# The second channel product of two token tiles by Strassen's algorithm, in a fused attention and mixer kernel in fp32

## The chip, the cores and the metric

The kernel is one program on 1 core of a Trainium2 chip. Its time is the device time of one execution in microseconds (us), the median of three runs. The engines are PE (TensorE, with PEld for its weight loads), DVE (VectorE), ACT (ScalarE), POOL (GpSimd, which here issues DMAs) and SP (SyncE, which issues most DMAs).

## The reference, cut to what matters

```python
# x: 4 batches x 448 tokens x 768, the result of sigmoid attention and a gated convolution
h  = np.maximum(xt @ w_tok1, 0.0) @ w_tok2          # mixes tokens, xt = x transposed
u  = x + h.transpose(0, 2, 1)
h2 = np.maximum(u @ w_ch1, 0.0) @ w_ch2             # w_ch1 768 x 1536, w_ch2 1536 x 768
out = (u + h2).astype(np.float32)
```

The change lies in the last two lines: `u @ w_ch1` is the first channel product, the product with `w_ch2` the second. There are 1792 tokens.

## The kernel before

The program runs through attention, the gated projections, the token mix and at last the channel products. It computes everything transposed: channels lie on the 128 partitions, tokens in the columns. An fp32 product is made of three matmuls on fp32r operands: every operand is split into a high part (ACT copies it to fp32r) and a low part (DVE subtracts the high part), and high x high, low x high and high x low are added in PSUM. An array of 768 channels has KD = 6 blocks of 128, the 1536 hidden channels have KF = 12 blocks, called `fc`.

The 1792 tokens go in four tiles of 512, 512, 384 and 384 (`TILES`), called 0 to 3. For tiles 0 and 1, `ch1(t, fc)` makes one block of hidden channels (18 matmuls, L745), splits its ReLU (`split`, L92 and L94), and `ch2(t, fc)` adds that block's share of all six output blocks in six PSUM banks (`pso`, tags `o0` to `o5`, 18 matmuls, L772). Their calls alternate, `ch2` one block behind `ch1`. After `fc` = 11 DVE adds `u` to each bank (L778, tile `ur`) and SP stores the sum.

For tiles 2 and 3 together the first channel product is made by Strassen's algorithm (in Winograd's form, seven block products instead of eight): the two tiles are the two columns of a block matrix, the two halves of the 768 input channels its rows, and the hidden blocks 2i and 2i+1 the two rows of the weights. What it needs is made beside tile 1, at places that `beside` lists by the block `fc` of `ch1(1, fc)`: `sums(i)` forms the four sums of weights for pair i on DVE and ACT and stores all seven operands in the HBM scratch `fscr` (L892, L912); `turned_load(k)` and `turned(k)` load u and form the seven operands of the tokens for block k of 3 (L932, L936, L940). Then `seven(i)` makes the seven products of pair i, 9 matmuls each (`product`, L976), in two PSUM banks (`h`), with weights that POOL loads from `fscr` six products ahead (`form_load`, L968, tiles `wf` in the six `xs` buffers), and DVE adds them up (L993).

The second channel product of tiles 2 and 3 is not by Strassen before: `ch2(2, fc)` follows each `seven`, two blocks behind, and `ch2(3, fc)` comes last, with hidden blocks that went to the scratch `rscr` and come back (`r_load`, `r_split`). Tiles 2 and 3 take 12 x 18 matmuls each there, on 384 columns.

From `with tc.manual_schedule()` on, each engine's order is the order of the code; ahead of it a scheduler sets it.

Of the kernel before, what the change touches and what calls it, by code (L numbers as in the profile page):

```python
# [34 lines left out]
def tile_kernel(ctx, tc, qT, kT, v, w_val, conv_w, w_out, w_tok1, w_tok2, w_ch1, w_ch2, out):  # L35
# [39 lines left out]
    rscr = dram.tile([KF, P, NJ], F32, name="rscr")  # L75

    def f(ap):
        return ap.bitcast(F32)
# [786 lines left out]
    with tc.high_priority(-CHAN_LOW):  # L865
        for fc in range(CHAN_HELD + 1, KF):
            dec_ch(fc)
    forms = ("a11", "s2", "s1", "s4", "s3", "a12", "a22")
    spot = {name: n for n, name in enumerate(("a11", "a12", "a22", "s1", "s2", "s3", "s4"))}
    room = []  # L870
    bform = {}

    def form_room():
        if not room:
            fc = form_room.at
            form_room.at += 1
            if 0 < fc < CHAN_LATE:
                get = w_tile if fc < CHAN_HELD else wo_tile
                room.extend(get().rearrange("p (c m) -> p c m", c=2) for _ in range(2))
            else:  # L880
                t = rp["p" if fc else "a"].tile([P, 2, 2, HALF], F32R, tag=f"wch{fc}_0", bufs=1, name="bf")
                room.extend(t[:, n] for n in range(2))
        return room.pop(0)

    form_room.at = 0

    def keep_weights(fc):
        for a in range(2):
            w = f(wch[fc][0][a])
            for n, h in enumerate((0, 1) if fc % 2 == 0 else (1,)):  # L890
                at = spot[("a11", "a12")[h] if fc % 2 == 0 else "a22"]
                nc.sync.dma_start(fscr[fc // 2, at, :, a], w[:, h * HALF : (h + 1) * HALF])  # L892

    def sums(i):
        keep_weights(2 * i)
        keep_weights(2 * i + 1)
# [4 lines left out]
        add = lambda o, x, y, op=ALU.add: nc.vector.tensor_tensor(out=o, in0=x, in1=y, op=op)  # L901
        for w, fc in ((wa, 2 * i), (wb, 2 * i + 1)):
            add(w, f(wch[fc][0][0]), f(wch[fc][0][1]))
        s = [f(su[:, n]) for n in range(4)]
        add(s[0], wb[:, :HALF], wb[:, HALF:])
        add(s[1], s[0], wa[:, :HALF], ALU.subtract)
        add(s[2], wa[:, :HALF], wb[:, :HALF], ALU.subtract)
        add(s[3], wa[:, HALF:], s[1], ALU.subtract)
# [4 lines left out]

    ub = {}

    def turned_load(k):
        at = [None] * 6
        if k == KH - 1:
            spare = [rp["a"].tile([P, 4, NJ], F32, tag="raw", bufs=2, name="ub") for _ in range(2)]
            at = [spare[n // 4][:, n % 4] for n in range(6)]  # L920
        ub[k] = [u_load(t, k + h, "ub", at[2 * n + t - 2]) for n, h in enumerate((0, KH)) for t in (2, 3)], at[4:]

    def turned(k):
        (b11, b12, b21, b22), t = ub.pop(k)
        if t[0] is None:
            t = [both.tile([P, W], F32, tag="gate", bufs=6, name="ut")[:, :NJ] for _ in range(2)]
        t1, t2 = t
        to = {}

        def high(name, src):  # L930
            to[name] = src, form_room()
            nc.scalar.activation(out=to[name][1][:, 0], in_=src, func=AF.Copy)  # L932

        def low(name):
            src, x = to.pop(name)
            nc.vector.tensor_tensor(out=x[:, 1], in0=src, in1=f(x[:, 0]), op=ALU.subtract)  # L936
            bform[name, k] = x

        def sub(o, x, y):
            nc.vector.tensor_tensor(out=o, in0=x, in1=y, op=ALU.subtract)  # L940

        high("b11", b11)
        sub(t1, b12, b11)
        high("t1", t1)
        low("b11")
        sub(t2, b22, t1)
# [4 lines left out]
        sub(b12, b22, b12)  # L951
# [4 lines left out]
        sub(t1, b21, t2)  # L956
# [4 lines left out]
    queue = [(i, name) for i in range(KF // 2) for name in forms]  # L961
    held_f = {}

    def form_load():
        if queue:
            i, name = queue.pop(0)
            t = both.tile([P, 2, HALF], F32R, tag="xs", bufs=KD, name="wf")
            nc.gpsimd.dma_start(t, fscr[i, spot[name]])  # L968
            held_f[i, name] = t

    def product(i, name, x):
        ps = psc.tile([P, 512], F32, tag="h", bufs=2, name="psm")[:, :NJ]
        w = held_f.pop((i, name))
        for k in range(KH):
            for n, (a, c) in enumerate(((0, 0), (1, 0), (0, 1))):
                nc.tensor.matmul(  # L976
                    ps, w[:, a, k * P : (k + 1) * P], bform[x, k][:, c],
                    start=k == 0 and n == 0, stop=k == KH - 1 and n == 2,
                )
        form_load()  # L980
        return ps

    def seven(i):
        def spare():
            return both.tile([P, W], F32, tag="gate", bufs=6, name="um")[:, :NJ]

        def out(ps):
            t = spare()
            nc.scalar.activation(out=t, in_=ps, func=AF.Copy)  # L989
            return t  # L990

        def add(o, x, y):
            nc.vector.tensor_tensor(out=o, in0=x, in1=y, op=ALU.add)  # L993

        m1 = out(product(i, "a11", "b11"))
        u = spare()
        add(u, product(i, "s2", "t2"), m1)
        m5 = out(product(i, "s1", "t1"))
        v = spare()
        add(v, u, m5)  # L1000
        add(v, product(i, "s4", "b22"), v)
        nc.sync.dma_start(rscr[2 * i], v)
        add(u, product(i, "s3", "t3"), u)
        add(m5, u, m5)
        nc.sync.dma_start(rscr[2 * i + 1], m5)
        r = rp["a"].tile([P, 2, 2, NJ], F32R, tag="raw", bufs=2, name="rr")
        add(m1, product(i, "a12", "b21"), m1)
        split(r[:, 0, 0], r[:, 0, 1], m1, relu=True)
        add(u, product(i, "a22", "t4"), u)
        split(r[:, 1, 0], r[:, 1, 1], u, relu=True)  # L1010
        for n in range(2):
            r_t[2, 2 * i + n] = [r[:, n, c] for c in range(2)]

    back = {}

    def r_load(fc):
        if fc < KF:
            back[fc] = both.tile([P, W], F32, tag="gate", bufs=6, name="rl")[:, :NJ]
            nc.sync.dma_start(back[fc], rscr[fc])

    def r_split(fc):
        if fc < KF:
            r = rp["p"].tile([P, 2, W], F32R, tag="r", bufs=2, name="r")
            r = [r[:, c, :NJ] for c in range(2)]
            split(*r, back.pop(fc), relu=True)
            r_t[3, fc] = r
# [10 lines left out]
    cut = order.index((ch2, 0, KF - 1)) + 1  # L1037
    for fn, t, fc in order[:cut]:
# [7 lines left out]
    with tc.manual_schedule():  # L1046
        beside = {1: (sums, 0), 2: (sums, 1), 3: (sums, 2), 4: (turned_load, 0, sums, 3), 5: (turned, 0)}
        beside |= {6: (sums, 4), 7: (turned_load, 1, sums, 5), 8: (turned, 1), 9: (turned_load, 2), 11: (turned, 2)}
        for fn, t, fc in order[cut:]:
            fn(t, fc)  # L1050
            if fn is ch1:
                todo = beside.get(fc, ())
                for n in range(0, len(todo), 2):
                    todo[n](todo[n + 1])
            if fn is ch1 and fc == KF - 1:
# [64 lines left out]
```

## Time and profile before

| | |
|---|---|
| median of three runs | 709.95 us (709.52 to 710.09) |
| the profiled execution, its own time | 710.43 us |
| span of its profile, first to last instruction | 708.7 us |
| instructions | 11027 |
| busy: PE, PEld | 701.8 us (99%), 574.3 us (81%) |
| busy: DVE, ACT, POOL | 481.0 us (68%), 305.4 us (43%), 88.9 us (13%) |
| DMA | 128.16 MB, mean 181 GB/s |

Times in the profile count from the start of the span. Shares of busy time are means over stages with different limits, so the stages are read one by one; the last 170 us, from the second half of tile 1 on, are those the change rewrites.

### The profile page before, as it was taken

The page shows a single profiled execution, that of the slowest core. Times are in us where ns is not written, and L with a number is a line of the kernel's source. Part 1 is how long each engine was busy: PE and PEld are TensorE (multiplying, and loading weights), DVE is VectorE, ACT ScalarE, POOL GpSimd, SP SyncE. Part 2 cuts the span into 40 slices and gives each one's busy share as a digit, 9 for nine tenths or more (in the row PEclk, how much of TensorE's full clock was granted, in tenths as well). Part 3 has the DMA queues.
Part 4 walks back from the last instruction along what each step waited for, and adds up shares of the span by engine and source line. Part 5 has one row for each costly group of instructions (what it writes and reads, how often), then busy time and mean ns, then how long its engine had stood idle before and what let it go on. Part 6 is the DMA issues. An engine that isn't in the chain of part 4 may idle for free.

```text
span 708.7 us, 11027 instructions
## 1 busy us (share of the span) xinstructions
PE 701.8 (99%) x4210; PEld 574.3 (81%) x4210; DVE 481.0 (68%) x789; ACT 305.4 (43%) x454; POOL 88.9 (13%) x128
## 2 busy tenths in 40 slices
PE   8999999999999999999999999999999999999997
PEld 3344444699999999999988888888888899999997
DVE  1799776479899988976878999747774543233222
ACT  5899888337426435524733344402322211111110
POOL 0000110003214212400350000000000232220000
PEclk9999999999999999999999999999999999999999
DMA  9847999413346333335895444337967696663533
GB/s 290 261 132 234 278 288 282 145 54 85 53 158 198 72 110 114 86 118 160 240 305 202 158 159 174 98 126 297 331 218 244 190 296 185 189 192 122 176 100 111
DMA packets 102212, 128.16 MB, mean 181 GB/s; under 512 B 35072, under 2 KB 89104, under 8 KB 102160
## 3 DMA queue, kind: packets, MB, share of 16 engines
q1 hardware_dynamic: 90672, 90.40, 42.3%
q0 software_dynamic: 11056, 36.61, 16.2%
q8 instruction: 33, 0.54, 0.3%
q10 hardware_dynamic: 432, 0.46, 0.2%
q14 instruction: 19, 0.16, 0.1%
HBM read 83.98 MB, written 37.16 MB: 171 GB/s over the span
## 4 chain that ended last, share of the span: by engine, by line
PE 93%; DVE 3%; DMA 2%; ACT 1%; issue 1%; SPq 0%; DVEq 0%; ACTq 0%
PE psd L359 24%; PE pso L772 23%; PE psh L745 12%; PE psm L976 9%; PE pss L281 9%; PE psy L296 8%; PE pst L423 4%; PE pst L436 4%; DMA raw<-w_ch 1%; ACT ga L283 1%; DMA k<-kT 0%; DMA out<-ur 0%; DVE dec_a L135 0%; DVE x2T L440 0%; DVE ub L940 0%
## 5 line engine op out<-in xcount | busy, mean ns | idle before, releaser
L283 ACT ACTIVATE ga<-pss,bias_s 128x896 f32<-128x896 f32 x84 | 83.4, 1003 | 19.9 <-PE pss L281 19.3
L359 PE MATMUL psd<-gv,wo 128*128 128x448 f32 x432 | 88.0, 362 | 0.0
L359 PE MATMUL psd<-xs,w 128*128 128x448 f32 x432 | 87.7, 362 | 0.0
L359 PEld LDWEIGHTS psd<-xs,w 128*128 128x128 f32 x432 | 80.8, 187 | 6.0 <-issue 0.7
L359 PEld LDWEIGHTS psd<-gv,wo 128*128 128x128 f32 x432 | 81.0, 187 | 5.4
L281 PE MATMUL pss<-q,k 64*64 64x448 f32 x672 | 79.1, 542 | 1.1 <-ACT ga L283 0.7
L296 PE MATMUL psy<-ga,v 64*64 64x448 f32 x672 | 77.6, 536 | 0.0
L329 DVE SCALAR_TENSOR_TENSOR gate<-xb,cw,gate 128x448 f32<-128x448 f32 x96 | 75.0, 781 | 2.6
L281 PEld LDWEIGHTS pss<-q,k 64*64 64x64 f32 x672 | 26.0, 134 | 40.2 <-issue 29.6
L296 PEld LDWEIGHTS psy<-ga,v 64*64 64x64 f32 x672 | 25.7, 133 | 37.4 <-issue 35.9
L968 POOL DMA_DIRECT2D wf<-fscr x42 | 22.2, 528 | 238.8 <-PE psh L745 167.1
L135 DVE SCALAR_TENSOR_TENSOR dec_a<-raw,dec_a 128x768 int32<-128x768 int32 (+2 forms) x38 | 33.5, 881 | 20.8 <-ACT dec_a L123 20.8
L123 ACT ACTIVATE dec_a<-dec_a,exp_b 128x768 int32<-128x768 int32 (+3 forms) x39 | 33.0, 858 | 33.0 <-DVE dec_a L120 33.0
L993 DVE TENSOR_TENSOR um<-psm,um 128x384 f32<-128x384 f32 x30 | 16.7, 556 | 43.9 <-PE psm L976 42.9
L394 POOL COPY pl<-st 128x1024 uint16<-128x1024 uint16 x21 | 30.7, 1460 | 103.9 <-ACT gate L340 50.8
L370 ACT ACTIVATE gv<-gate 128x448 fp32r<-128x448 f32 x24 | 13.9, 578 | 56.8 <-DVE gate L368 56.7
L976 PE MATMUL psm<-bf,wf 128*128 128x384 f32 x162 | 35.9, 335 | 0.3 <-ACT um L989 0.3
L94 DVE SCALAR_TENSOR_TENSOR r<-psh,r 128x512 fp32r<-128x512 f32 x22 | 15.0, 688 | 30.3 <-ACT r L92 30.3
L772 PE MATMUL pso<-r,wo 128*128 128x512 f32 (+1 forms) x162 | 35.0, 371 | 0.0
L772 PEld LDWEIGHTS pso<-r,wo 128*128 128x128 f32 x162 | 29.6, 188 | 4.2
L772 PE MATMUL pso<-r,w 128*128 128x512 f32 (+1 forms) x144 | 30.9, 369 | 0.0
L92 ACT ACTIVATE r<-psh 128x512 fp32r<-128x512 f32 x22 | 12.9, 591 | 40.9 <-PE psh L745 40.9
(200 smaller groups left out, 1282.7 us busy)
## 6 DMA issues: line engine op xcount, KB each, us to landing
raw<-w_ch SPq DMA_DIRECT2D x24, 768.0 KB, 4.4
wf<-fscr POOLq DMA_DIRECT2D x42, 384.0 KB, 4.7
v<-v SPq DMA_DIRECT2D x24, 224.0 KB, 6.4
uscr<-x2T POOLq DMA_DIRECT2D x24, 224.0 KB, 2.4
q<-qT SPq DMA_DIRECT2D x23, 224.0 KB, 4.5
k<-kT SPq DMA_DIRECT2D x22, 224.0 KB, 4.6
raw<-w_out POOLq DMA_DIRECT2D x6, 768.0 KB, 8.1
fscr<-sum_h SPq DMA_DIRECT2D x6, 768.0 KB, 3.4
```

The lines of the kernel that those rows point to most:

```text
L123: nc.scalar.activation(out=t["a"], in_=t["a"], func=AF.Relu, scale=8.0, bias=exp_b)
L135: nc.vector.scalar_tensor_tensor(out=t["a"], in0=hi, scalar=-0x80000000, in1=t["a"], op0=ALU.bitwise_and, op1=ALU.bitwise_or)
L281: nc.tensor.matmul(ps[cols, j, :S], k[rows, keys], q[rows], start=True, stop=True)
L283: nc.scalar.activation(out=a, in_=ps[:, :, :S], func=AF.Sigmoid, bias=bias_s, scale=QK_SCALE)
L296: nc.tensor.matmul(y_t[i + h][cols, :S], v_t[i][rows, c, cols], a[rows, j], start=c == 0, stop=c == NB - 1)
L329: nc.vector.scalar_tensor_tensor(out=acc, in0=x[:, t : t + S], scalar=w, in1=acc, op0=ALU.mult, op1=ALU.add)
L359: nc.tensor.matmul(ps[:, :S], w(a, kk), s[:, c, :], start=kk == 0 and n == 0, stop=kk == KD - 1 and n == 2,)
L394: nc.gpsimd.tensor_copy(back.rearrange("p (n h) -> p h n", h=2), st.rearrange("p h c d -> p h (c d)"))
L423: nc.tensor.matmul(ps[:, :HALF], a, x[:, m], start=n == 0, stop=n == len(mm) - 1)
L745: nc.tensor.matmul(ps[:, :n_t], wch[fc][0][a][:, kk * P : (kk + 1) * P], us_t[t, kk][:, c, :], start=kk == 0 and n == 0, stop=kk == KD - 1 ...
L772: nc.tensor.matmul(acc[j][:, :n_t], wch[fc][1][a][:, j * P : (j + 1) * P], r[c], start=fc == 0 and n == 0, stop=fc == KF - 1 and n == 2,)
L976: nc.tensor.matmul(ps, w[:, a, k * P : (k + 1) * P], bform[x, k][:, c], start=k == 0 and n == 0, stop=k == KH - 1 and n == 2,)
```

## The change

The second channel product of tiles 2 and 3 is also made by Strassen's algorithm: `second(j)` makes output blocks j and j + 3 of both tiles by seven products of 18 matmuls (six pairs of hidden blocks, three matmuls each), for j = 0, 1, 2. That is 3 x 7 x 18 = 378 matmuls on 384 columns in place of 432; `ch2(2, ...)`, `ch2(3, ...)`, `rscr`, `r_load` and `r_split` are gone. The pairs of hidden blocks are now f and f + 6.

- `sums_second(i)`, new: DVE forms the operands of the second weights for pair i (two sums of 128x768, four of 128x384) and SP stores seven operands in the new scratch `gscr`, laid out so that a product can load one block. Each store moves 128 x 3 runs of 128 floats (512 bytes).
- `first_pairs(i)` replaces `seven(i)`: all six pairs come one after the other, with no `ch2` between them. It adds up the products, takes the ReLU, and forms the seven operands of the hidden blocks (`rform`), each split in a high and a low part; the last of these steps run beside the next pair (`tail`).
- `second(j)` loads its weights unsplit (`load_2`), and ACT and DVE split them (`split_2`: 128x768 each), three products ahead.
- `bank` deals out all eight PSUM banks in turn, `h` and then `o0` to `o5`.
- `beside` is rewritten; `sums_first(0)` and `sums_second(0)` move ahead of tile 1, `keep_first` of blocks 5 to 11 goes to POOL's queue, and tile 1's `ur` lies in `raw` buffers.

```diff
-        beside = {1: (sums, 0), 2: (sums, 1), 3: (sums, 2), 4: (turned_load, 0, sums, 3), 5: (turned, 0)}
-        beside |= {6: (sums, 4), 7: (turned_load, 1, sums, 5), 8: (turned, 1), 9: (turned_load, 2), 11: (turned, 2)}
+        beside = {
+            1: [(sums_first, 1), (keep_first, 0, nc.sync), (keep_first, 1, nc.sync)],
+            2: [(sums_first, 2), (keep_first, 2, nc.sync), (keep_first, 3, nc.sync)],
+            3: [(sums_first, 3), (keep_first, 4, nc.sync)],
+            4: [(turned_load, 0), (sums_second, 1)],
+            5: [(turned, 0)],
+            6: [(sums_first, 4)],
+            7: [(turned_load, 1), (sums_first, 5)],
+            8: [(turned, 1)],
+            9: [(turned_load, 2), (sums_second, 2), (sums_second, 3, True)],
+            10: [(sums_second, 4), (sums_second, 5, True)],
+            11: [(turned, 2)],
+        }
...
+    def sums_second(i, other=False):
...
+        for n in range(2):
+            add(w[n], f(wch[i + n * HK][1][0]), f(wch[i + n * HK][1][1]))
+        four([su[:, n] for n in range(4)], w[0][:, :HALF], w[1][:, :HALF], w[0][:, HALF:], w[1][:, HALF:])
+
+        def keep(name, x):
+            dst = gscr[spot[name], :, :, i].rearrange("j p m -> p j m")
+            nc.sync.dma_start(dst, x.rearrange("p (j m) -> p j m", j=KH))
+
+        keep("a11", w[0][:, :HALF])
+        keep("a12", w[1][:, :HALF])
+        keep("a22", w[1][:, HALF:])
+        for n in range(4):
+            keep(f"s{n + 1}", su[:, n])
...
+    def split_2():
+        if cut_2:
+            key = cut_2.pop(0)
+            t = joint((0, 9, 10, 11)[len(cut_2) % 4], 0, [P, 2, DM])
+            nc.scalar.activation(out=t[:, 0], in_=raw_2[key], func=AF.Copy)
+            add(t[:, 1], raw_2.pop(key), f(t[:, 0]), ALU.subtract)
+            held_2[key] = t
...
+    def bank():
+        n = bank.n % 8
+        bank.n += 1
+        if n < 2:
+            return psc.tile([P, 512], F32, tag="h", bufs=2, name="psm")[:, :NJ]
+        return pso.tile([P, 512], F32, tag=f"o{n - 2}", name="psn")[:, :NJ]
...
+    def first_pairs(i, tail):
+        def go(name):
+            ps = product(held_1.pop((i, name)), [bform[pairs[name], k] for k in range(KH)])
+            load_1()
+            for fn in tail.pop(0) if tail else ():
+                fn()
+            return ps
...
+        add(u, go("a22"), u)
+        relu(u)
+        high("b21", u)
...
+    def second(j, tail):
+        def go(name):
+            ps = product(held_2.pop((j, name)), [rform[pairs[name], i] for i in range(HK)])
+            load_2()
+            split_2()
+            for fn in tail.pop(0) if tail else ():
+                fn()
+            return ps
...
+                if fc == KF - 2:
+                    for n in range(2):
+                        at = rp["a"].tile([P, KH, W], F32, tag="raw", bufs=2, name="ur")
+                        for m in range(KH):
+                            ur[t, KH * n + m] = u_load(t, KH * n + m, "ur", at[:, m])
...
-        for i in range(KF // 2):
-            seven(i)
-            if i:
-                for fc in (2 * i - 2, 2 * i - 1):
-                    ch2(2, fc)
...
+        tail = []
+        for i in range(HK):
+            if i == HK - 1:
+                last = first_pairs(i, tail)
+            else:
+                tail = first_pairs(i, tail)
+        tail = [sum(last, [])]
+        for _ in range(3):
+            split_2()
+        for j in range(KH):
+            second(j, tail)
```

How the change moves instructions is shown at three places. The first is SP's queue late in tile 1, from the loads of the last block of tokens (`ub`) to the stores of tile 1's result (`out`). Before:

```order
L912 DMA fscr<-sum_s 128x4x384
L725 DMA ub<-uscr 128x320
L725 DMA ub<-uscr 128x64
L725 DMA ub<-uscr 128x384
...
L725 DMA ur<-uscr 128x384
L725 DMA ur<-uscr 128x128
...
L780 DMA out<-ur 128x512 x6
```

Now:

```order
L726 DMA ub<-uscr 128x384
L949 DMA gscr<-sum_w 128x3x128 x3
L949 DMA gscr<-sum_s 128x3x128 x4
L949 DMA gscr<-sum_a 128x3x128
L949 DMA gscr<-sum_b 128x3x128 x2
L949 DMA gscr<-form 128x3x128 x4
...
L726 DMA ur<-uscr 128x384
L726 DMA ur<-uscr 128x128
...
L781 DMA out<-ur 128x512 x6
```

The five rows of `gscr` stand twice, for pairs 2 and 3 and for pairs 4 and 5: 28 stores now come between the loads of `ub` and the 12 loads of `ur`, which followed each other before.

The second place is ACT's queue where the first channel product of tiles 2 and 3 ends and the second begins (`w`, `wo` and `form` are room for operands, `wg` are raw weights of the second product). Now:

```order
L1054 ACTIVATE um<-um 128x384
L1068 ACTIVATE w<-um 128x384
L1022 ACTIVATE form<-wg 128x768 x4
L1068 ACTIVATE wo<-um 128x384
L1068 ACTIVATE wo<-uv 128x384
L1068 ACTIVATE w<-uc 128x384
```

The first two rows are the ReLU and the high part of the last product of the last pair; the four copies of weights for `second(0)` stand behind them, and the high parts of pair 5's sums behind these.

The third is DVE at the same place. Now:

```order
L904 TENSOR_TENSOR um<-psm,um 128x384
L904 TENSOR_TENSOR form<-wg,form 128x768 x4
L904 TENSOR_TENSOR w<-um,w 128x384
L904 TENSOR_TENSOR um<-um,uv 128x384
L904 TENSOR_TENSOR uv<-uv,uc 128x384
```

The first row takes the last product of pair 5 from its bank; the low parts of the four weights of `second(0)` come next, and then pair 5's remaining sums. Before, nothing but the split of two hidden blocks (`rr`) stood there, two blocks ahead of the `ch2` that read it.

## Rows read from the trace of the kernel before

**Rows 1.** The page, part 1: busy time, share, instructions by engine.

```profile
PE 701.8 (99%) x4210; PEld 574.3 (81%) x4210; DVE 481.0 (68%) x789; ACT 305.4 (43%) x454; POOL 88.9 (13%) x128
```

**Rows 2.** Waits of PE, whole span: us, times, longest.

```profile
PE psm L976 <- ACT um L989: 0.3, 1, 0.3
```

**Rows 3.** The chain that ended last, 480 to 710 us: start, length, what.

```profile
551.39 4.09 PE psh L745 x18
...
567.10 19.01 PE psm L976 x108
...
592.35 10.92 PE psm L976 x63
...
654.75 50.16 PE pso L772 x288
...
704.93 0.56 DVE ur L778
```

**Rows 4.** DVE's timeline, 540 to 600 us: start, length, operation, [idle before].

```profile
539.88 0.69 DVE L94 SCALAR_TENSOR_TENSOR r<-psh,r 128x512 fp32r<-128x512 f32 x1 [1.40 <-ACT r L92]
...
556.14 0.69 DVE L94 SCALAR_TENSOR_TENSOR r<-psh,r 128x512 fp32r<-128x512 f32 x1 [7.41 <-ACT r L92]
...
562.54 3.67 DVE L778 TENSOR_TENSOR ur<-pso,ur 128x512 f32<-128x512 f32 x6
```

**Rows 5.** Stretches: PE, PEld, DVE, ACT, POOL, clock, DMA share, GB/s.

```profile
540.00:545.00 5.00, 5.00 (x24) 4.14 (x23) 0.57 (x1) 0.00 (x0) 0.00 (x0) 1.00 0.91 258
...
555.00:560.00 5.00, 5.00 (x24) 4.14 (x23) 3.73 (x8) 2.59 (x6) 1.05 (x2) 1.00 1.02 297
...
570.00:575.00 5.00, 5.00 (x30) 5.00 (x30) 2.43 (x6) 0.52 (x1) 1.58 (x3) 1.00 1.10 335
```

**Rows 6.** DVE and ACT groups, 480 to 710 us; a row of ACT's timeline.

```profile
L993 DVE TENSOR_TENSOR um<-psm,um 128x384 f32<-128x384 f32 x30 | 16.7, 556 | 43.9 <-PE psm L976 42.9 <-ACT um L989 0.9
...
L901 DVE TENSOR_TENSOR sum_a<-wo 128x768 f32<-128x768 f32 x2 | 1.9, 948 | 0.0
...
L92 ACT ACTIVATE rr<-um 128x384 fp32r<-128x384 f32 x12 | 6.3, 525 | 35.4 <-DVE um L993 35.4
...
426.52 0.85 ACT L153 ACTIVATE wch__3851<-dec_a 128x768 fp32r<-128x768 f32 x1 [0.91 <-DVE dec_a L135]
```

**Rows 7.** DMA, 42 to 46.5 us (`v`): packets, MB, share.

```profile
q1 hardware_dynamic: 928, 0.46, 36.0%
```

**Rows 8.** DMA, 552 to 562 us (six loads of `wf`).

```profile
q0 software_dynamic: 857, 2.34, 78.9%
```

**Rows 9.** DMA, 540 to 545 us (loads of `ur`).

```profile
q1 hardware_dynamic: 1370, 1.29, 90.5%
```

**Rows 10.** The page, part 6: DMA issues, KB, median us.

```profile
out<-ur SPq DMA_DIRECT2D x12, 192.0 KB, 2.0
```

**Rows 11.** DMA, 482 to 486 us (stores in runs of 1536 bytes).

```profile
q1 hardware_dynamic: 1082, 1.60, 106.6%
```

**Rows 12.** Timelines of DVE and PE at the start of tile 1.

```profile
454.86 3.41 DVE L98 TENSOR_TENSOR us<-u,us 128x512 fp32r<-128x512 f32 x5 [2.46 <-ACT us L92]
...
458.83 0.68 DVE L98 TENSOR_TENSOR us<-u,us 128x512 fp32r<-128x512 f32 x1
...
461.47 4.24 PE L745 MATMUL psh<-us,wch__3249 128*128 128x512 f32 x18
```

**Rows 13.** PE's timeline, 0 to 14 us.

```profile
1.16 3.17 PE L795 MATMUL psi<-zero 128*128 128x448 bf16 x8 [1.16 <-DVE zero L784]
4.64 2.60 PE L281 MATMUL pss<-q,k 64*64 64x448 f32 x16 [0.31 <-DMA k<-kT]
...
12.00 0.93 PE L296 MATMUL psy<-ga,v 64*64 64x448 f32 x8
```

**Rows 14.** `wf` loads issued at 594.21 and 602.01: KB, us to landing.

```profile
wf<-fscr POOLq DMA_DIRECT2D x1, 384.0 KB, 3.4
...
wf<-fscr POOLq DMA_DIRECT2D x1, 384.0 KB, 5.6
```

More of the change, by code (lines that the diff above doesn't have):

```diff
@@ new lines, in tile_kernel, with add, four @@
+    halves = []
+    b_room = rooms([(0, 0, 2)] + ["w"] * 6 + ["wo"] * 6 + [(fc, 0, 2) for fc in (9, 10, 11)] + [(7, 0, 1)])
+    r_places = [(0, 1, 2)] + ["w"] * 6 + ["wo"] * 6 + [(fc, 1, 2) for fc in range(7, 12)] + [(8, 0, 2), "half"]
+    r_places += ["r", "r", "raw", "raw", "dec_a", "dec_c", "w", "w", "w", "wo", "wo", "w", "wo"]
+    r_room = rooms(r_places)
+    def add(o, x, y, op=ALU.add):
+        nc.vector.tensor_tensor(out=o, in0=x, in1=y, op=op)
+    def four(s, a11, a12, a21, a22):
+        add(s[0], a21, a22)
+        add(s[1], s[0], a11, ALU.subtract)
+        add(s[2], a11, a21, ALU.subtract)
+        add(s[3], a12, s[1], ALU.subtract)
@@ L950, in turned @@
         low("t2")
-        sub(b12, b22, b12)
+        add(b12, b22, b12, ALU.subtract)
         high("t3", b12)
@@ L955, in turned @@
         low("t3")
-        sub(t1, b21, t2)
+        add(t1, b21, t2, ALU.subtract)
         high("t4", t1)
@@ L959, in turned, with load_1 @@
         low("t4")
[L961 to L966, printed above, removed]
+    turn_1 = ("a11", "a12", "s2", "s1", "s4", "s3", "a22")
+    turn_2 = ("a11", "s1", "s2", "s4", "s3", "a12", "a22")
+    queue_1 = [(i, name) for i in range(HK) for name in turn_1]
+    queue_2 = [(j, name) for j in range(KH) for name in turn_2]
+    cut_2 = list(queue_2)
+    held_1, held_2, raw_2 = {}, {}, {}
+    def load_1():
+        if queue_1:
+            i, name = queue_1.pop(0)
@@ L967, in form_load, with load_2 @@
             t = both.tile([P, 2, HALF], F32R, tag="xs", bufs=KD, name="wf")
             nc.gpsimd.dma_start(t, fscr[i, spot[name]])
[L969 to L974, printed above, removed]
+            held_1[i, name] = t
+        else:
+            load_2()
+    def load_2():
+        if queue_2:
+            j, name = queue_2.pop(0)
+            t = both.tile([P, DM], F32, tag="xs", bufs=KD, name="wg")
+            nc.gpsimd.dma_start(t, gscr[spot[name], j].rearrange("p f m -> p (f m)"))
+            raw_2[j, name] = t
@@ L981, in product @@
         return ps
[L983 to L1026, printed above, removed]
+    def spare(name):
+        return both.tile([P, W], F32, tag="gate", bufs=6, name=name)[:, :NJ]
@@ L1037, in tile_kernel @@
     cut = order.index((ch2, 0, KF - 1)) + 1
+    with tc.high_priority(-CHAN_LOW):
+        for fc in range(CHAN_HELD + 1, KF):
+            dec_ch(fc)
+            keep_first(fc, nc.gpsimd)
+        sums_first(0)
+        sums_second(0)
     for fn, t, fc in order[:cut]:
```

209 lines of the change are left out of this document (137 added, 72 removed).

## The prediction

> **What bounds the kernel now.** I read the page's busy times first: PE works 99% of the span, DVE, the next, 68% [rows 1]. Then PE's waits: after the start the longest is 0.3 us, at the first products of tiles 2 and 3 [rows 2]. So the time is PE's work, and fewer matmuls shorten it as far as nothing else makes PE wait. The chain that ended last shows the price of a matmul on 384 columns [rows 3]: 63 of the first product take 10.92 us, the last 288 of the second 50.16, so 173 and 174 ns. Behind the last stands one DVE add and a store, which stay. Then I read what runs beside PE late in tile 1, where the change puts new work: DVE stood idle for 7.41 us ahead of the split of block 11 at 556.14 [rows 4], and the 16 DMA engines are 91% busy at 540 us, full at 555 and at 110% at 570, where two queues work at once [rows 5].
>
> **The change part by part.**
>
> *Matmuls.* The order shows 54 fewer on 384 columns. 54 x 173.3 ns (10.92 / 63) = 9.36 us, all on the path. The 0.3 us wait goes too: it was for a buffer that tile 1's `ur` held, which now lies in `raw`, and the products now have eight banks. Together -9.66.
>
> *DVE late in tile 1.* `sums_second` is two operations of 0.95 us and four of 0.555 [rows 6], 4.1 at most. Beside `fc` = 9 and 10 stand two pairs each: with 0.6 for the split of r, 8.8 in a period of two blocks, 8.16 (4.09 and 4.08 a block [rows 3]). Over the two periods the split of block 11 comes 1.3 us late, near 557.4; `ch2(1, 11)` needs it at 551.39 + 4.09 + 4.08 = 559.56. `turned(2)` lies between that split's end and the adds at 562.54 [rows 4], 5.8 us, and now ends near 563.9; the second product of pair 0, now a12, needs its tenth result near 566.2. Both are hidden with over 2 us to spare, unless a sum waits for its buffer.
>
> *Transfers late in tile 1.* This can cost most. Four pairs store 28 times, from the split at 539.88 on [rows 4], and SP issues the loads of `ur` only behind these. Tile 1's adds need `ur`, and they free the banks `o0` to `o5`; the third product of pair 0 is the first to take one. Without a stall PE starts it at 559.56 + 4.08 + 2 x 1.56 = 566.76 (9 x 173 ns = 1.56). A pair is 7 x 384 = 2688 packets of 512 bytes. The trace has no such store; its loads of `v` have packets of that size: 928 held 36.0% of 16 engines for 4.5 us, 27.9 ns each [rows 7]. So a pair takes 2688 x 27.9 / 16 = 4.69 us of all engines, four 18.8. The six loads of `wf` ahead of the first product fall in the same time: 78.9% of 10 us, 7.9 [rows 8]. One `ur` block, 256 packets at 52.8 ns (1370 in 90.5% of 5 us [rows 9]), takes 0.8. That is 27.5 us from 539.88 + 0.6 + 0.95 = 541.4, to 568.9. A store of 192 KB lands 2.0 us after its issue [rows 10]; I take 1.5 of it as no transfer; the add takes 0.7 [rows 4]. Bank free at 571.1: a wait of 4.3 us. Where two queues overlap as at 570 (1.10 [rows 5]), the work takes 25.0 and the wait is 1.8. I take 3.0, since the queues overlap for a part of it. Bounds: at the rate of stores of 1536 bytes (1.60 MB in 4 us, 401 GB/s [rows 11]) the 5.5 MB take 13.7 us and the wait is 0; at 52.8 ns a packet, the mean of a mix of longer packets, they take 35.5 and the wait is 21. The packet of equal size is nearest. +3.0.
>
> By the Trainium skill (DMA: Bandwidth & Descriptors, Specifications) a transfer reaches line rate from 512 bytes a run, which these stores just meet; by that this term would be 0 and the sum 704.4. The loads of `v`, at 512 bytes in 27.9 ns, 18.4 GB/s an engine against 25 for the stores of 1536 bytes (401 / 16), don't bear that out.
>
> *From the first product to the second.* Before, `ch2` of older blocks stood here. Now, with T the end of the last product of pair 5, the order leaves a chain: DVE adds it (0.56), ACT takes the ReLU (0.53) and the high part (0.53), then the first weights' high part (128x768: 0.85) [rows 6]: 2.5 us in which PE has nothing. The second matmul needs the low part: DVE 0.95, less one matmul, +0.8. Then a11 runs; s1 needs the low part of pair 5's t1, which stands on DVE behind four weights' low parts and eight operations of 0.55, at T + 10.1, against T + 3.3 + about 35 matmuls, T + 9.35: +0.75. Sum +4.1. In this order it can't be less than 2.5; if DVE falls behind in the pairs, each us of lag adds one.
>
> *The six pairs in a row.* DVE has 18 operations of 128x384 a pair, 18 x 0.555 = 10.0 us beside 10.92 of PE. Eight banks let PE run ahead, so waits of DVE for ACT are hidden; a lag left at the end is priced above. POOL now loads `wf` every 1.56 us without the breaks that `ch2` gave. The first 14 products of before ran back to back, 108 and more matmuls with no wait [rows 3]. Taken as 0; the bound on the other side is a rival.
>
> *Start of tile 1.* `sums_first(0)` (4.1 us, and its split of 128x1536, estimated as twice 0.95 on DVE and twice 0.85 on ACT [rows 6]) now stands among the splits of tile 1's u. The last of those ended at 459.5 and is needed at 461.47 + 5/6 x 4.24 = 465.0 [rows 12], 5.5 later. 6.0 + 1.7 less the 2.46 us in which DVE idled there: 5.2 at most. Hidden, with little to spare. The stores of blocks 5 to 11 are in POOL's queue, which issues nothing urgent until `wf`.
>
> *Second product.* For seven products, 21.8 us of PE, DVE has 7 x 0.95 + 11 x 0.55 = 12.7 and ACT 7 x 0.85 + 2 x 0.53 = 7. Hidden. The end is as before: one add, one store.
>
> Sum: -9.66 + 3.0 + 4.1 = -2.6 on the profiled execution's 710.43, which is 0.5 above the median of 709.95. Against the median I forecast 707.4 us.
>
> **The rivals.**
>
> *The transfers make way in time.* The wait at the third product is 0, and 709.95 - 9.66 + 4.1 = 704.4. For it: long stores at 401 GB/s, and an SP queue that can keep two stores in flight. Against: 27.5 us of work in 25.
>
> *The stores of 512 bytes hold up tile 1's end.* If a packet takes 35 ns, four pairs take 23.5, and with `wf` and `ur` 32.2: bank free at 575.8, a wait of 9. With 8.5 us lost, and one slow restart as below (2.3), 709.95 - 9.66 + 8.5 + 4.1 + 2.3 = 715.2. It decides from a wait of 5.6 us at the third product on: then nothing is left of the gain. For it: DMA already stood at 100% and more in two of the stretches read [rows 5].
>
> *PE restarts slowly after a wait.* At the start of the program 8 matmuls on 448 columns take 3.17 us, 396 ns each, and 16 of the scores 2.60, where 8 later take 0.93 [rows 13]. At the pace of the 173 ns for 384, 448 columns would take 202 ns: 396 is half speed, the 1.2 GHz level of the clock against 2.4. This start cost 8 x 0.194 = 1.5 us and 2.60 - 1.86 = 0.7, together 2.3. One such fall, after the wait at either place, gives 709.7; two give 712.0. In the stretches read late in the kernel the granted clock is 1.00 [rows 5] and no wait is over 0.3 us, so no row shows a fall after a wait.
>
> By the Trainium skill (TensorE: Matmul & The Clock Gate, Part 1) an array that has idled is throttled to half rate and has to earn the full rate by sustained work. No run here shows it within the kernel; by that rule this rival's 709.7 is the result.
>
> *The stream of `wf` falls behind* once 42 products follow each other. For it: a load issued at 594.21 landed after 3.4 us, one issued at 602.01, five products later, after 5.6 [rows 14]: 0.44 more per load. Over 36 loads that is 16 us, less five products of slack, 7.8, plus two slow restarts and the two terms above: 709.95 - 9.66 + 8 + 7.1 + 4.6 = 720. Against: the 14 products in a row before.
>
> **How the numbers follow.** The forecast with a wait of 1.8 to 4.3 us at the third product (706.2 to 708.7) gets 0.36, the clean case 0.20, the slow restart 0.17, the held-up end 0.20, the stream 0.07. A measurement of this kernel tells 0.2%, 1.4 us, from no change: faster is below 708.5, slower above 711.4. Faster: 0.20 + 0.32 of the forecast = 0.52. Same: 0.04 of the forecast and 0.12 of the restart, 0.16. Slower: the held-up end, the stream and 0.05 of two restarts, 0.32. The range leaves out the stream, the worst of the held-up end and a little below the clean case: 703.8 to 716.0. The likeliest case's own range is 706.2 to 708.7.
>
> **What the profile will show.** The matmuls on 384 columns at 173 ns, 54 fewer. A wait of PE at the third product for a DVE add into `ur`, and behind it for loads of `ur`: 2 to 4 us if I am right, none or over 5.6 if a rival is. At the border of the products a wait of PE for ACT's `form<-wg` of 2.5 us, then shorter ones for DVE. DMA at full share from 541 to 569. The granted clock below 1.00 after either wait would show the slow restart. I am wrong if PE waits for `wf`, for the splits of tile 1's u near 461, or nowhere at all.

## The result, and the profile after

The changed kernel takes 713.72 us (median of 20 runs, 710.09 to 719.81), the kernel before 709.69 us (20 runs, 709.09 to 710.56): a ratio of 1.0059, with a 95% interval of 1.0039 to 1.0078. It is slower by some 4 us where 2.5 less were forecast. The times also spread over 10 us instead of 1.5, and every run had a mean granted clock below 1 (0.987 to 0.998), where the kernel before has 0.999 or 1.0 in every run that stands beside the experiments.

The profiled execution of the changed kernel took 715.29 us, its span is 713.5. First the busy times, from the page, to set beside [rows 1]:

```profile
PE 697.2 (98%) x4156; PEld 567.8 (80%) x4156; DVE 553.7 (78%) x909; ACT 343.7 (48%) x523; POOL 110.9 (16%) x165
```

The 54 matmuls are gone (4210 to 4156), but PE is busy only 4.6 us less. The chain that ended last gives the price of the new products, one row for all:

```profile
602.65 9.36 PE psn L1039 x54
```

That is 173.3 ns, as in [rows 3]. So the gain of 9.36 us is there, and it is lost again elsewhere. PE's timeline shows where (start, length, line and operands; in brackets the idle time before and its releaser). Shown are the rows with a wait behind 400 us, and three more: the start of pair 0's first product (566.87), the row from which the pace is full again (580.64), and the last matmul ahead of the border (639.75):

```profile
463.45 0.73 PE L746 MATMUL psh<-us,wch__3249 128*128 128x512 f32 x2 [0.34 <-ACT us L93]
465.32 0.96 PE L746 MATMUL psh<-us,wch__3249 128*128 128x512 f32 x3 [1.15 <-DVE us L99]
466.52 2.58 PE L746 MATMUL psh<-us,wch__3249 128*128 128x512 f32 x10 [0.23 <-DVE us L99]
...
566.87 0.69 PE L1039 MATMUL psm<-form,wf 128*128 128x384 f32 x3
...
574.78 1.33 PE L1039 MATMUL psn<-w,wf 128*128 128x384 f32 x3 [4.60 <-DVE ur L779]
...
580.64 0.69 PE L1039 MATMUL psn<-w,wf 128*128 128x384 f32 x3
...
639.75 0.34 PE L1039 MATMUL psm<-form,wf 128*128 128x384 f32 x1
642.58 0.44 PE L1039 MATMUL psn<-form 128*128 128x384 f32 x1 [2.49 <-ACT form L1022]
643.58 0.64 PE L1039 MATMUL psn<-form 128*128 128x384 f32 x2 [0.55 <-DVE form L904]
...
650.42 0.45 PE L1039 MATMUL psn<-wo,form 128*128 128x384 f32 x1 [0.64 <-DVE wo L904]
```

PE waits at three places: in the first product of tile 1, at the third product of pair 0, and at the border of the two channel products. Behind the second of them more is lost than the wait. The stretches there, with the columns of [rows 5]:

```profile
566.80:574.70 7.90, 3.38 (x20) 3.02 (x18) 0.67 (x2) 0.49 (x1) 1.05 (x2) 0.94 1.11 341
574.70:581.20 6.50, 6.42 (x22) 6.42 (x23) 4.76 (x9) 1.41 (x3) 0.62 (x2) 0.55 1.05 332
581.20:639.90 58.70, 58.70 (x340) 58.57 (x338) 48.86 (x95) 32.28 (x68) 20.02 (x38) 1.00 0.89 250
639.90:644.00 4.10, 1.06 (x5) 0.61 (x4) 1.99 (x3) 4.04 (x8) 0.72 (x2) 1.00 0.84 321
```

From 574.7 to 581.2 the granted clock is 0.55 in the mean, near its 1.2 GHz level: 18 matmuls from 574.78 to 580.64 take 5.86 us for 18 x 0.173 = 3.12. PE stood still when the clock fell, and it came back while PE worked without a gap. So 2.74 us go there.

By the starts of the rows, the account of this execution is:

| part | us |
|---|---|
| 54 matmuls less; the wait of [rows 2] gone | -9.36, -0.3 |
| tile 1 starts later: 462.26 against 461.47 [rows 12] | +0.8 |
| its first product: 18 matmuls take 6.68 to the next block at 468.94, 4.08 without waits | +2.6 |
| the third product: 566.87 to 574.78, less 18 x 0.173 | +4.8 |
| the clock behind it | +2.7 |
| the border: 639.92 to 642.58, then 0.83 and 0.80 about the rows at 643.58 and 650.42 | +4.3 |

Together that is +5.5; the span grew by 4.8, with small gains between and at the end. The later start is of this execution: with the same kernel tile 1 starts at 461.39 in e11.

What the trace shows of the first wait: DVE's timeline, and one row of ACT's.

```profile
455.94 0.96 DVE L145 SCALAR_TENSOR_TENSOR wch__3848<-raw,dec_c 128x768 fp32r<-128x768 f32 x1
...
457.41 0.95 DVE L904 TENSOR_TENSOR sum_a<-wch__3249 128x768 f32<-128x768 f32 x1
...
460.79 0.56 DVE L904 TENSOR_TENSOR sum_s<-sum_a,sum_s 128x384 f32<-128x384 f32 x1
461.27 0.68 DVE L99 TENSOR_TENSOR us<-u,us 128x512 fp32r<-128x512 f32 x1
462.91 1.76 DVE L904 TENSOR_TENSOR sum_s<-sum_s,sum_h 128x1536 fp32r<-128x1536 f32 x1 [0.95 <-ACT sum_h L927]
464.58 0.68 DVE L99 TENSOR_TENSOR us<-u,us 128x512 fp32r<-128x512 f32 x1
```

```profile
461.39 1.49 ACT L927 ACTIVATE sum_h<-sum_s 128x1536 fp32r<-128x1536 f32 x1 [4.20 <-DVE sum_s L904]
```

All of `sums_first(0)` stands ahead of five of the six splits of tile 1's u, and it starts only at 457.41, when DVE has decoded the last weight. ACT's queue has the same order: its copy of the sums waits 4.20 us for DVE, and five of its six copies of u stand behind it.

Of the second, SP's timeline and a row of DVE's:

```profile
559.61 8.57 SPq L949 DMA_DIRECT2D gscr<-form  x4
568.23 6.94 SPq L726 DMA_DIRECT2D ur<-uscr  x12
```

```profile
574.03 1.29 DVE L779 TENSOR_TENSOR ur<-pso,ur 128x512 f32<-128x512 f32 x2 [7.65 <-DMA ur<-uscr]
```

SP is held 8.6 us by pair 5's last stores; the first loads of `ur` are issued at 568.23, and DVE, idle for 7.65 us, adds the first at 574.03. At the third place stands the order that the prediction read: four copies of raw weights on ACT behind the last ReLU. What of this is the cause, the experiments tell.

### The profile page after: what moved, and what is told of

Same layout as the page of the kernel before. It is cut to its first block, busy times and chain, and to the rows that moved or that the text cites. A ratio compares the mean times of both kernels' runs of the same rounds, so it can differ in the third digit from the quotient of the medians.

```text
span 713.5 us, 11250 instructions
## 1 busy us (share of the span) xinstructions
PE 697.2 (98%) x4156; PEld 567.8 (80%) x4156; DVE 553.7 (78%) x909; ACT 343.7 (48%) x523; POOL 110.9 (16%) x165
## 4 chain that ended last, share of the span: by engine, by line
PE 79%; DVE 12%; DMA 4%; ACT 2%; issue 1%; SPq 0%; DVEq 0%; ACTq 0%
PE psd L360 24%; PE psn L1039 14%; PE pss L282 9%; PE psy L297 8%; PE psh L746 7%; PE pso L773 6%; PE pst L424 4%; PE psm L1039 4%; DMA raw<-w_ch 3%; PE pst L437 3%; DVE dec_a L136 2%; DVE raw L131 2%; DVE dec_a L121 1%; DVE r L95 1%; DVE dec_c L142 1%
## 5 line engine op out<-in xcount | busy, mean ns | idle before, releaser
L282 PEld LDWEIGHTS pss<-q,k 64*64 64x64 f32 x672 | 26.3, 135 | 39.9 <-issue 29.6
L1039 PE MATMUL psn<-form 128*128 128x384 f32 x165 | 32.4, 335 | 3.0 <-ACT form L1022 2.5
L1039 PEld LDWEIGHTS psn<-form 128*128 128x128 f32 x165 | 28.8, 188 | 3.6 <-ACT form L1022 2.8
L904 DVE TENSOR_TENSOR form<-wg,form 128x768 fp32r<-128x768 f32 x21 | 19.8, 955 | 13.3 <-ACT form L1022 13.3
L424 PE MATMUL pst<-x,wt1H 128*128 128x384 f32 x112 | 29.9, 336 | 0.0
L1022 ACT ACTIVATE form<-wg 128x768 fp32r<-128x768 f32 x21 | 17.4, 843 | 23.8 <-PE psn L1039 19.6
L131 DVE SCALAR_TENSOR_TENSOR raw<-raw,dec_c 128x768 f32<-128x768 uint32 (+2 forms) x32 | 27.9, 873 | 1.0
```

The costliest lines, as they stand in the source:

```text
L131: nc.vector.scalar_tensor_tensor(out=lo.bitcast(F32), in0=lo.bitcast(U32), scalar=2.0**-32, in1=t["c"], op0=ALU.mult, op1=ALU.add)
L282: nc.tensor.matmul(ps[cols, j, :S], k[rows, keys], q[rows], start=True, stop=True)
L424: nc.tensor.matmul(ps[:, :HALF], a, x[:, m], start=n == 0, stop=n == len(mm) - 1)
L1039: nc.tensor.matmul(ps, w[:, a, k * P : (k + 1) * P], x[:, c], start=k == 0 and n == 0, stop=k == len(xs) - 1 and n == 2,)
```

## The experiments

Kernels of one group (e1 to e4, e5 to e8, e9 to e11) ran on one chip beside the kernel before; ratios are to that, with their 95% intervals.

**e1: PE kept busy in the wait.** In `first_pairs`, pair 0's second product runs four times:

```diff
-            ps = product(held_1.pop((i, name)), [bform[pairs[name], k] for k in range(KH)])
+            ps = product(held_1.pop((i, name)), [bform[pairs[name], k] for k in range(KH)], 4 if (i, name) == (0, "a12") else 1)
```

> The 9 matmuls of pair 0's second product (a12) run four times over into the same bank, 27 more, 27 x 0.173 = 4.7 us of work where PE stood idle for 4.6 us before the third product; nothing else changes, and each repeat starts the sum anew. Theory A: the clock fell because PE stood still (granted 0.50 for 6.8 us in the changed kernel's profile, 18 matmuls in 5.86 us for 3.12). Then the granted clock stays at 1.00 over the third product, and the time is 2.7 us below the changed kernel's 713.7, about 711.0, with less spread, since the runs with a lower mean clock are the slower ones. Rival: the fall comes from something else at that place (the change to new banks and weights, or the transfers). Then the clock falls all the same and the time stays at 713.7 or above.

Measured: 712.26 us (ratio 1.0040, 1.0028 to 1.0051), 711.32 to 713.61. Stretches of its profile:

```profile
566.00:570.00 4.00, 4.00 (x25) 4.00 (x24) 0.00 (x0) 0.49 (x1) 0.53 (x1) 1.00 1.09 319
574.00:578.00 4.00, 4.00 (x25) 4.00 (x24) 3.41 (x7) 1.29 (x3) 1.07 (x3) 1.00 1.00 314
640.00:644.00 4.00, 3.84 (x14) 3.84 (x15) 3.93 (x7) 1.51 (x3) 2.15 (x4) 0.61 0.55 167
```

With work in the gap the clock stays at 1.00 over the third product, though the transfers and the new banks are the same. One profile alone would be thin, but all seven that have the wait there (the change, e2, e3, e4, e6, e7, e11) show a fall behind it, and none of the five without the wait (e1, e5, e8, e9, e10) does. That excludes the rival for this place. The size was wrong: 0.7 us below the changed kernel on the same chip (e11, 712.98), within the two intervals, not 2.7. In the profiled execution the clock fell at the border instead (0.61); and the 4.7 us of added work are more than the wait that they fill where it is short (3.35 in e11).

**e2: stores in long runs.**

```diff
-    gscr = dram.tile([7, KH, P, HK, P], F32, name="gscr")
+    gscr = dram.tile([7, P, HK, KH, P], F32, name="gscr")
...
-            dst = gscr[spot[name], :, :, i].rearrange("j p m -> p j m")
+            dst = gscr[spot[name], :, i]
...
-            nc.gpsimd.dma_start(t, gscr[spot[name], j].rearrange("p f m -> p (f m)"))
+            nc.gpsimd.dma_start(t.rearrange("p (f m) -> p f m", f=HK), gscr[spot[name], :, :, j])
```

> The scratch of the second weights is laid out so that a store has runs of 1536 bytes instead of 512, and the loads of the second product have runs of 512 bytes instead of 3072. Theory A: the wait of 4.8 us at the third product is the transfers of tile 1's end, priced by the 512-byte packet. The 5.5 MB of the four pairs then take 13.7 us instead of 18.8 or more, the wait is about 0, the clock does not fall, and the time is 4.8 + 2.7 = 7.5 us lower: about 706.2. The loads of the second product, 768 packets of 27.9 ns, 1.3 us of all engines in each 3.12 us, stay hidden. Rival: what is late is the order (DVE forms pair 5 only at 560 us, and the loads of ur stand behind its stores whatever their length). Then at most the part of the packets goes, the wait stays at 3 us or more, and the time is above 709.

Measured: 712.31 us (1.0051, 1.0033 to 1.0069). A miss for theory A. PE's timeline at the third product, and SP's ahead of it:

```profile
572.78 0.79 PE L1039 MATMUL psn<-w,wf 128*128 128x384 f32 x3 [2.94 <-DVE ur L779]
```

```profile
558.52 2.67 SPq L949 DMA_DIRECT2D gscr<-form  x4
561.24 12.30 SPq L726 DMA_DIRECT2D ur<-uscr  x12
```

SP is free 7 us earlier, but the loads then take longer: two that were issued before 566 us took 9.0 to land. At 566 to 570 the engines stood at 1.10 with 387 GB/s. The stores of pairs 4 and 5, six blocks of `wf` and twelve loads of `ur` all fall behind 551 us, when DVE starts on these sums; a shorter store moves the queue, not its end. So the length of the runs is not what sets this wait. The rival, the place of `ur` in the order, is left; e5 tests it.

**e3 and e7: the border.** e3 puts two splits ahead in pair 5:

```diff
         relu(c12)
+        if i == HK - 1:
+            split_2()
         add(u, go("s3"), u)
         add(c22, u, c22)
         relu(c22)
+        if i == HK - 1:
+            split_2()
         high("b22", c22)
-        add(u, go("a22"), u)
-        relu(u)
-        high("b21", u)
+        ps = go("a22")
...
+        if i == HK - 1:
+            tail_1()
+            tail_2()
+            low("t1")
+            add(u, ps, u)
+            relu(u)
+            high("b21", u)
+            split_2()
+            return [[lambda: low("t2"), tail_3, lambda: low("t4")]]
...
-        for _ in range(3):
-            split_2()
```

> The splits of the first two second weights move ahead of the last products of pair 5 (after s4 and after s3), and pair 5's t1 ahead of its other sums; no operation is added or left out. Theory A: PE's 3.7 us at the border of the two products (2.5, 0.55 and 0.64 us) are the order on ACT and DVE alone. They shrink to 0.5 us or less: about 3.2 us below 713.7, 710.5. Rival: the raw second weights have not landed by then (POOL asks for the first of them only when pair 5's second product ends, some 8 us ahead, and a load took 4.1 us in the median). Then PE waits for DVE's first-weights split or for pair 5's last sums by 1.5 us or more, and the time is 712 or above.

Measured: 712.57 us (1.0049, 1.0032 to 1.0065). PE's waits from 600 us on (total, times, longest):

```profile
PE psn L1039 <- ACT form L1022: 1.9, 1, 1.9
PE psn L1039 <- DVE form L904: 0.6, 1, 0.6
```

The first two products start without a wait. The third waits, because its split stood behind the ReLU of the last sum. Of 3.7 us 2.5 stayed: the rival's size, but not its reason. e7 gives that split its own place (`split_high` is ACT's part of `split_2` and returns DVE's):

```diff
         high("b22", c22)
+        if i == HK - 1:
+            third = split_high()
         ps = go("a22")
...
             low("t1")
+            third()
             add(u, ps, u)
             relu(u)
             high("b21", u)
-            split_2()
```

> As e3, with the third split (s2's weights) also ahead: ACT's part behind the ReLU of s3's sum, DVE's part behind pair 5's t1. In e3 the wait at the first two products was gone and one of 1.9 + 0.55 us came back at the third, for ACT's split behind the ReLU of the last sum. Theory A: it is order alone, and the waits of the border now sum to 0.6 us or less: 3.1 below 713.7, about 710.6. Rival: the third raw weights land too late (a load took 5.5 us there in e3, and POOL's first three issues came 3.6 us late). Then 1.5 us of wait or more stay, at the third or the fourth product.

Measured: 711.89 us (1.0023, 1.0007 to 1.0038), and from 600 us on:

```profile
PE psn L1046 <- DVE wo L904: 0.7, 1, 0.7
PE psn L1046 <- DVE form L904: 0.5, 2, 0.3
```

3.7 us of waits have become 1.2. The raw weights had landed; it was order.

**e4 and e6: the start of tile 1.** The written order begins earlier, and the sums move behind the splits of u:

```diff
-    cut = order.index((ch2, 0, KF - 1)) + 1
+    cut = order.index((None, 0, KF - 1))
...
-        sums_first(0)
-        sums_second(0)
...
+            if fn is None:
+                for j in range(KD):
+                    del us_t[t, j]
+                    prep_load(t + 1, j)
+                    prep_split(t + 1, j)
+                sums_first(0)
+                continue
             fn(t, fc)
-            if fn is ch1:
+            if fn is ch2 and (t, fc) == (0, KF - 1):
+                sums_second(0)
+            if fn is ch1 and t:
```

> The weight sums of pair 0 move behind the splits of tile 1's u: sums_first(0) right behind them, sums_second(0) behind tile 0's last adds; the stretch from there on is in written order. Theory A: PE's waits of 0.3, 1.15 and 0.2 us at the first product of tile 1, with the delay in it 2.6 us, are DVE's sums ahead of the splits. They go: 711.1. Rival: the splits are late because the weights are decoded later (DVE ends that at 456.8 us, 451.7 before the change, with the stores of the first weights beside its loads). Then moving the sums gains under 1 us. Either way the sums now stand among later work of DVE; if that makes the end of tile 1 later, the wait at the third product grows and eats the gain.

Measured: 731.17 us (1.0314, 1.0294 to 1.0333). PE's waits for u were gone, but tile 0's adds came late. SP's timeline tells why:

```profile
472.44 0.34 SPq L781 DMA_DIRECT2D out<-ur  x1
472.82 0.93 SPq L726 DMA_DIRECT2D ur<-uscr  x2
477.73 0.34 SPq L781 DMA_DIRECT2D out<-ur  x1
478.11 0.94 SPq L726 DMA_DIRECT2D ur<-uscr  x2
```

In written order each load of `ur` stood behind the store of the sum before it, and PE waited five times for a bank. That was an error of the experiment, and it says nothing of the sums. e6 adds one line ahead of `sums_first(0)`: `ur_load(0)`.

> As e4, but with all loads of ur for tile 0 issued at once, ahead of the sums' stores. In e4 each load stood behind the store of the one before it on SP, and tile 0's banks came free 4 us apart (13 us of waits); the wait for the splits of tile 1's u was gone. Theory A: with the loads ahead, both waits are gone: 2.6 us below 713.7, 711.1, and up to 1.7 more where the clock fell at that place. Rival: sums_first(0) and its split stand ahead of tile 0's adds on DVE, and they free the banks 1 us or more late: no gain.

Measured: 711.79 us (1.0020, 1.0003 to 1.0036). PE's waits from 440 us on:

```profile
PE psn L1039 <- DVE ur L779: 2.7, 1, 2.7
PE psn L1039 <- ACT form L1022: 2.5, 1, 2.5
PE pso L773 <- DVE r L95: 1.0, 2, 0.6
```

No wait for u is left: theory A. DVE's timeline has the splits right behind the decode:

```profile
458.46 3.09 DVE L99 TENSOR_TENSOR us<-u,us 128x512 fp32r<-128x512 f32 x5
```

The decode ends as late as in the change (456.98 is its last operation's start, 455.94 there), so a late decode alone does not make PE wait. The run moves two things at once, the sums and the start of the written order; their shares are not told apart.

**e5: `ur` ahead of the last stores.**

```diff
-            10: [(sums_second, 4), (sums_second, 5, True)],
+            10: [(sums_second, 4, 2), (sums_second, 5, True)],
...
-                for todo, *args in beside.get(fc, ()):
-                    todo(*args)
                 if fc == KF - 2:
...
+                for todo, *args in beside.get(fc, ()):
+                    todo(*args)
```

The 2 gives pair 4's sums the room of weights that are done (`joint(7, 1)`, `joint(8, 1)`), so that `raw` is free for `ur`.

> The loads of ur for tile 1 are issued ahead of the stores of pairs 4 and 5; pair 4's sums lie in other room so that ur need not wait for them. The stores, their length and DVE's work stay as in the change. Theory A: tile 1's adds wait for the loads of ur alone (in e2, with stores three times as long, they were issued at 561 us, landed 9 us later beside the loads of wf, and 2.9 us of wait stayed). Then the wait at the third product is 0 and with it goes the fall of the clock there: 4.8 + 2.7 lower than 713.7, about 706.2, or 708 where the falls at the two other waits stay. Rival: the same bytes then delay the loads of wf (2.4 MB behind the stores), and PE waits for wf at the first products by 2 us or more: 709 or above.

Measured: 708.85 us (0.9981, 0.9969 to 0.9994). SP now issues the loads at 555.07, ahead of the stores of pairs 4 and 5:

```profile
555.07 6.81 SPq L726 DMA_DIRECT2D ur<-uscr  x12
```

Its stretches:

```profile
464.50:470.00 5.50, 4.35 (x12) 2.92 (x11) 5.50 (x9) 2.07 (x5) 0.00 (x0) 0.69 0.87 267
566.00:574.00 8.00, 8.00 (x44) 7.53 (x43) 6.63 (x12) 2.46 (x5) 1.23 (x3) 1.00 1.14 350
```

From 566 to 574 PE works without a gap at 1.00, with the same stores in 512-byte runs and DMA at 1.14. The change at 1.0059 becomes 0.9981: 0.0078 x 709.7 = 5.5 us, between the wait alone (4.8) and the wait with its fall of the clock (7.5). So the order of the loads on SP is what made this wait. PE did not wait for `wf` there. The fall of the clock at the start of tile 1 stayed (0.69).

**e8: all four edits.**

> The edits of e2, e5, e6 and e7 together. Theory A (the matmuls gain 9.4 us, and the three places with waits, with the falls of the clock behind them, give it all back): no wait over 0.6 us stays behind the start, the granted clock is 1.00 throughout, and the time is 709.7 - 9.4 + about 1 = 701.3, with a spread of a microsecond as before the change. Rival: PE then waits somewhere else, because DVE and the DMA engines have no room left in tile 1 or in the pairs: 704 or above.

Measured: 702.96 us (702.70 to 704.21; 0.9903, 0.9889 to 0.9918): 0.97% faster than before the change. All its waits from 380 us on:

```profile
PE psn L1050 <- DVE form L904: 0.8, 2, 0.6
PE psn L1050 <- DVE wo L904: 0.7, 1, 0.7
PE pso L773 <- DVE r L95: 0.3, 1, 0.3
PE psn L1050 <- DMA wf<-fscr: 0.2, 1, 0.2
```

The mean clock is 0.999 to 1.0 in every run, and the spread is 1.5 us again. 701.3 was expected, with about 1 us of waits; the 2.0 that are left account for 1.0 of the 1.7 above it, the rest is open. The gains of e5, e6 and e7 over the change, 5.5, 2.8 and 2.6 us, add up to 10.9; that of e8 is 0.0156 x 709.7 = 11.1. So the three places together are the loss, as far as the intervals tell.

**e9 and e10: taking back one edit of e8.** e9 has the stores in short runs again, e10 the border in the change's order.

> e8 with the scratch of the second weights as in the change: stores in runs of 512 bytes again, loads of the second product in runs of 3072. The three orders stay mended. Theory A: what the 512-byte stores cost is a wait for ur, and with ur loaded ahead it is hidden: the time is e8's 703.0 within 1 us. Rival: the 512-byte stores hold up the loads of wf behind them (e8 already shows 0.24 us for one), PE waits for wf and in some runs the clock falls: 704.5 or above.

Measured: 703.87 us (0.9915, 0.9903 to 0.9928), 0.9 above e8 with overlapping intervals: within theory A's bound. Its longest wait for `wf` is 0.5 us. Whether the long runs help at all stays open at this size.

> e8 with the border of the two products in the change's order, so that the three waits there (2.5, 0.55 and 0.65 us in the changed kernel) are the only ones left. Theory A: a wait costs itself, and behind it in some runs a stretch at half the clock. The time is 703.0 + 3.7 less the 0.6 of e8's own border, 1.3 in its profile: about 705.5 in the runs without a fall and 1.5 to 2 more in those with one, the mean clock 0.998 or lower in these. Rival: the clock falls only behind the longer wait at the third product; then every run is within 1 us of 705.5 and the clock 0.999 or more.

Measured: 704.84 us (0.9935, 0.9923 to 0.9946), 1.9 above e8, the mean clock of its five runs 0.994, 0.998, 0.998, 0.998 and 1.0. PE's longest waits:

```profile
PE psn L1043 <- ACT form L1026: 2.5, 1, 2.5
...
PE psn L1043 <- DVE wo L904: 0.7, 1, 0.7
PE psn L1043 <- DVE form L904: 0.6, 1, 0.6
```

The waits cost what theory A gave, 704.84 against 705.5. The rival's 0.999 in every run is excluded, but theory A's 1.5 to 2 us more are not there either: two of the runs at 0.998 took 704.04 and 704.56, less than the one at 1.0. The profiled run was that one, so where the clock fell in the others is not seen here; the profiles of e1 and e11 show a fall at the border.

**e11: the change again.**

> The changed kernel itself, as it stands, beside the others on the same chip: 713.7 as before, between 710 and 720, the mean clock between 0.987 and 0.998 and lower in the longer runs. If it is below 712 here, the gains of the other runs, taken from 713.7, are too large by as much.

Measured: 712.98 us (1.0052, 1.0033 to 1.0072), 711.27 to 716.36, clock 0.987 to 0.998, the longest run at 0.987. The change is as slow here as at first (1.0059); the gains above, taken from that, hold within 1 us. In its profile the clock fell at two places, the third product and the border:

```profile
570.00:574.00 4.00, 1.19 (x4) 1.19 (x5) 0.84 (x2) 0.00 (x0) 0.29 (x1) 0.82 1.07 321
574.00:578.00 4.00, 4.00 (x20) 4.00 (x19) 2.69 (x5) 0.00 (x0) 0.59 (x2) 0.76 1.08 383
...
638.00:642.00 4.00, 2.04 (x7) 1.78 (x8) 2.61 (x3) 3.53 (x6) 1.03 (x2) 0.85 0.61 226
642.00:646.00 4.00, 4.00 (x19) 4.00 (x18) 3.86 (x8) 1.58 (x3) 1.12 (x3) 0.72 0.95 318
```

## Why the prediction was wrong

The forecast was 707.4 and faster; the kernel takes 713.7 and is slower. That this lies inside the range is luck: the range reached so far for the held-up end with a wait of 9 us, which did not come. Two terms that the sum put at nothing failed, the start of tile 1 (2.6 us) and the clock (2.7 us), and a third, the wait at the third product, was 1.8 too small (4.8 for 3.0).

*Matmuls, -9.66: right.* 54 fewer at 173.3 ns.

*Start of tile 1, "Hidden, with little to spare": the step that failed first.* Priced at 0, it cost 2.6 us in the profile, and e6, which mends it alone, is 0.0039 x 709.7 = 2.8 us faster than the change (by the two intervals, 1.8 either way). The working had two faults. It let the sums begin in DVE's old idle time of 2.46 us; they begin behind the last decoded weight, and that now comes 5.1 us later (455.94). Before, the same operation stood here:

```profile
450.84 0.96 DVE L144 SCALAR_TENSOR_TENSOR wch__3848<-raw,dec_c 128x768 fp32r<-128x768 f32 x1
```

From 380 to 460 us DVE waits 4.2 us for raw weights (`raw<-w_ch`), before 0.2. The new stores of first weights run beside these loads, which is the likely reason; no run takes them away. The second fault: it took 5.2 of 5.5 us for hidden, where a miss by one operation decides.

*Clock, the restart "once" a rival at 709.7: it should have been part of the sum.* It was priced at 2.3 and cost 2.74 behind the third product in the profile. That price came from the start of the program, where matmuls take twice their time but the granted clock reads 1.00 in the trace, so there the half speed is inferred from durations; behind the third product the granted clock itself shows it. Nor is it one fall. Besides the third product, where seven of seven profiles with a wait have it, the profiles show it at the start of tile 1 in three of seven with waits there (e2, e3, e5) and behind the 2.5 us at the border in three of eight (e1, e4, e11). The mean clock of 0.998 or less says that each of the 20 runs of the change has one or more. The longer runs mostly have the lower clock (0.987 in the two longest), so this is part of why the time spreads; it is not all, since seven runs at 0.995 go from 710.1 to 715.3, and the wait at the third product differs too (4.60 in the profile, 3.35 in e11). With waits of 2 to 4 us forecast at two places, a chance of 0.17 was too low. The Trainium skill (TensorE: Matmul & The Clock Gate, Part 1) says that an idle array is throttled to half rate until it has worked for a while; the 0.55 from 574.7 to 581.2 us agrees, and e1, where PE did not idle, has 1.00 at that place.

*Third product, +3.0 out of 1.8 to 4.3: right in place and path, low in size, and wrong in what sets the size.* The wait was 4.60 (4.58 in e7), but 3.35 in e11, 3.06 in e3 and 2.75 in e6: the nominal 4.3, from transfers without overlap of the queues, is nearer in two profiles, 3.0 in three. The price of the packet held:

```profile
q1 hardware_dynamic: 1931, 0.95, 105.8%
```

This is DMA from 552 to 555 us, stores alone but for one packet: 1.058 x 16 x 3 us / 1931 = 26.3 ns a packet, 27.9 estimated from [rows 7]. But the sum's remedy was wrong: it would have made the wait 0 for long stores, and e2 had 2.9. It counted one block of `ur` where all twelve loads share the engines with `wf`, and it let transfers begin before their sums exist. The bound of 0 held only by another order (e5). So the Trainium skill's rule of line rate from 512 bytes (DMA: Bandwidth & Descriptors, Specifications) was not the question here; the trace doesn't bear it out, 320 GB/s for these stores against 401 for the longer ones [rows 11]. The rival of the held-up end took 8.5 into its sum where its own wait is 9.0; with that it stands at 715.7, and it did not come either way.

*Border, +4.1: right.* 3.7 us of waits, 2.49 of them the chain of 2.5 that was read from the order, 4.3 by the starts. e7, which mends it alone, is 2.6 us faster than the change (1.0059 to 1.0023, 1.8 either way).

*Six pairs in a row, taken as 0: right.* From 581.2 to 639.9 PE is busy without a gap, so the rival of the `wf` stream didn't come. *DVE late in tile 1* was hidden as forecast, with both ends late: block 11's split started at 559.91 (557.4 worked out), needed at 562.79 (559.56).

The sum with what was left out, +2.6 for the start and +2.7 for the clock, is 707.4 + 5.3 = 712.7; with 4.8 for the third product it is 714.5. The median of 713.7 lies between.

## What to carry to other kernels

In a kernel where PE is 99% busy, work taken off PE counts in full only if no new wait of PE is left anywhere; here three short ones, with the fall of the clock behind one, took back more than the 9.4 us, and mending their order made the same change 0.97% faster than before. Price a wait of PE with the chance of a stretch at half the clock behind it, and look for it in the spread and in the mean clock of the runs. Where a step is moved ahead of a split that PE waits for, price it from the time at which it starts in the new order, and issue loads with a deadline ahead of stores that have none.

## What was not expected of the hardware

The same kernel with the same wait shows a fall of the clock in one execution and none in another: behind the 2.5 us at the border there is none in the profile of the change (1.00 from 639.9 to 644.0) and one in e11 (0.72). And a fall can follow shorter waits: in e5 it comes at the start of tile 1 (0.69), where the longest is 1.15 us. What decides it stays open; no run was made for it. Within one kernel this is part of what makes runs of 710 and of 720 us.
